# Queries of the opening put off, and unread matmuls in idle array time, in a two-layer transformer prompt kernel

## The chip, the cores and the metric

The kernel runs on one core of one Trainium2 chip. The metric is the time of one execution in device microseconds. All runs quoted here are fast (none was over 1.5% above the fastest of its kernel in its call); a kernel was run several times, and medians are given with their extremes. The calls ran on different chips, so a kernel is compared with the runs of the kernel before that were made beside it, and across calls only by its ratio to those. The granted clock is the share of TensorE's full clock that the profile records.

## The reference, cut to what matters

Two identical layers over x of 2048 x 448 in bfloat16. Each is an attention with 16 heads of 28, over all 2048 keys without a mask, and a dense part of width 1792 with a squared ReLU, each behind a layernorm.

```python
x = x + A(layernorm(x), wqkv, wo)     # softmax(q k^T / sqrt(28)) v, then @ wo
x = x + B(layernorm(x), w1, b1, w2, b2)   # relu(x @ w1 + b1)**2 @ w2 + b2
x = x + A(layernorm(x), wqkv, wo)     # the same weights again
x = x + B(layernorm(x), w1, b1, w2, b2)
```

The softmax needs 2 x 16 x 2048 x 2048 exponentials: 134 million. ScalarE does them all, in 683 instructions of up to 128 x 1536.

## The kernel before

The kernel is written as several streams of operations (scores, exponentials, products with the values, the chain from the attention's output to the next layer's queries), each operation with an engine, an estimated duration and what it depends on. A planner in Python, run when the kernel is built, picks at each step the operation that can start first, and so fixes the order of instructions on each engine. On the chip that order stands, and an engine that comes too early waits: at 186.52 us of the kernel before VectorE has stood 4.23 us before a product whose reciprocals had not landed, and the eviction planned behind it starts at 187.13 us.

```python
LAT = {"PE": 0.22, "ACT": 0.22, "DVE": 0.10, "POOL": 0.15, "DMA": 2.0}

class Planner:
    def run(self):
        ...
            s, _, e, st = min(cands, key=lambda c: (c[0], c[1]))   # earliest start, then priority
            ...
            o.start, o.end = s, s + o.dur
            self.clock[e] = o.end
            if e == "PE":
                self.mode = o.mode
            o.fn(e) if o.fn else None          # emits the instructions
```

A score group is three matmuls of 32 rows (one head each) into a tile of 1536 columns in PSUM, where the kernel puts TensorE's results; the exponential reads the whole tile in one instruction; three matmuls of 32 columns then multiply by the values. There are two such score tiles, one tile of 512 columns, here called a bank, for the attention's output, and one, here called the spare bank, for all other matmuls. The kernel lets a bank take the next result only when another engine has read the last one out; that is called its eviction. At 187.87 us of the kernel before TensorE had waited 3.58 us for one. The streams of scores and exponentials, cut:

```python
def s_stream():
    ...
        o = gbuf[gi]["s"] = Op("PE", 0.23 + 0.04 * mm, fn, deps=list(deps), acq=R_sc, mode="row", sets=("s", gi))
def e_stream():
    ...
        nc.scalar.activation(out=pt[:, 0:n], in_=gbuf[gi]["sc"][:, 0:n], func=AF.Exp, scale=scale)
```

The softmax's denominators of a query block (except the last one of each layer) take a round trip through memory: out to 16 columns per partition, a reciprocal, out to DRAM (`scr<-dn`), and back, spread over the partitions (`rec<-scr`); then VectorE multiplies. The planner holds the last step to take 1.0 us plus 2.0 us until it has landed:

```python
def norm_stream(l, qb, g, res, oe):
    ...
        d1 = Op("DMA", 0.1, spread, deps=[oe])
        r1 = Op("DVE", 0.25, rcp, deps=[d1])
        d2 = Op("DMA", 0.1, away, deps=[r1])
        r = own = Op("DMA", 1.0, back, deps=[d2], acq=R_rec)
    ...
    m = Op("DVE", 0.1 + n / 960, mul, deps=[r], rel=oe)
```

In the opening, blocks of 512 rows of the first layer project keys of one group of heads, all values, the other keys, and then the queries:

```python
        else:
            yield from turned(*ks[0])
            yield from values()
            for a in [*ks[1:], *qs]:
                yield from turned(*a)
        yield Op("DVE", 0.0, None, deps=[last], rel=own_xt)
```

The softmax here doesn't subtract the row's maximum and nothing guards it: scores larger than these inputs give would overflow.

## Time and profile before

| | before |
|---|---|
| median of the first three runs | 1009.54 us (1006.92 to 1010.85) |
| profiled run, span | 1011.8 us |
| exponentials, ScalarE | 683, busy 924.6 us |
| first exponential starts, last ends | 24.1 us, 980.4 us |
| ScalarE waits for scores | 28.6 us in 38 pieces |
| mean granted TensorE clock | 0.895 |

A line of the profile's list of groups gives the source line, the engine, the operation, what is written and read, how often, then busy time and the mean of one, and after the second bar how long the engine stood idle just before these instructions and what ended that. In a timeline a line gives start and length in us, engine, line, operation and count, and in brackets the idle time before it and who ended it. A busy TensorE says little, since its matmuls overlap (four that begin at 697.89 us take 1.89, and the next begin at 699.71); the question is always how long ScalarE, which is the bound with 924.6 us of exponentials in 1011.8, stands idle, and where.

One more view of the kernel before is worth showing, because it shows how short the gaps were where the clock fell. It is the timeline of TensorE as it leaves the first layer's projections behind and has attention alone to do:

```profile
130.97 0.40 PE L502 MATMUL sc<-Q_sb,K_sb 32*128 32x512 bf16 x3 [0.47 <-ACT pt L517]
...
132.32 0.39 PE L502 MATMUL sc<-Q_sb,K_sb 32*128 32x512 bf16 x3 [0.62 <-ACT pt L517]
...
135.00 0.61 PE L502 MATMUL sc<-Q_sb,K_sb 32*128 32x512 bf16 x3 [0.62 <-ACT pt L517]
```

The gaps are 0.47 to 0.62 us, one in each period of about 1.34 us; after four of them the same three matmuls take 0.61 us instead of 0.39. Later, from 843.2 to 872 us, the clock stayed at 0.50 while tiled matmuls of attention alone filled 25.2 of 28.8 us.

### The profile page before, as it was taken

The page shows a single profiled execution, that of the slowest core. Times are in us where ns is not written, and L with a number is a line of the kernel's source. Part 1 is how long each engine was busy: PE and PEld are TensorE (multiplying, and loading weights), DVE is VectorE, ACT ScalarE, POOL GpSimd, SP SyncE. Part 2 cuts the span into 40 slices and gives each one's busy share as a digit, 9 for nine tenths or more (in the row PEclk, how much of TensorE's full clock was granted, in tenths as well). Part 3 has the DMA queues.
Part 4 walks back from the last instruction along what each step waited for, and adds up shares of the span by engine and source line. Part 5 has one row for each costly group of instructions (what it writes and reads, how often), then busy time and mean ns, then how long its engine had stood idle before and what let it go on. Part 6 is the DMA issues. An engine that isn't in the chain of part 4 may idle for free.

```text
span 1011.8 us, 15410 instructions
## 1 busy us (share of the span) xinstructions
PE 907.4 (90%) x6400; PEld 311.0 (31%) x6400; DVE 416.8 (41%) x929; ACT 943.9 (93%) x712; POOL 5.1 (1%) x14
## 2 busy tenths in 40 slices
PE   6989988898988988899898999898898998899998
PEld 2333322233232332233323333222233332233345
DVE  6644425424354154542545514225414510343254
ACT  4999998899999999999999999998899999999982
POOL 2000000000000000000000000000000000000000
PEclk7999967899989989899798998767997996679989
DMA  8000010000000000000000000010000000000000
GB/s 249 15 1 1 1 41 4 12 12 12 12 5 8 13 12 12 1 1 1 1 1 1 1 2 1 12 44 12 12 25 13 6 25 16 18 7 12 15 6 19
DMA packets 19730, 16.72 MB, mean 17 GB/s; under 512 B 8394, under 2 KB 16139, under 8 KB 19660
## 3 DMA queue, kind: packets, MB, share of 16 engines
q1 hardware_dynamic: 19660, 15.74, 5.0%
q8 instruction: 50, 0.82, 0.3%
q14 instruction: 20, 0.16, 0.1%
HBM read 13.47 MB, written 2.05 MB: 15 GB/s over the span
## 4 chain that ended last, share of the span: by engine, by line
ACT 45%; PE 21%; issue 17%; DMA 10%; DVE 6%; SPq 0%; ACTq 0%; DVEq 0%
ACT pt L517 45%; PE mt L385 8%; DMA rec<-scr 6%; PE sc L502 5%; PE oT L548 4%; PE sc L385 2%; DMA scr<-dn 2%; PE tp L350 2%; DMA dn<-oT_sb 1%; DVE r L673 1%; DVE rec L595 1%; DVE oTn L633 1%; DMA x_sb<-in_A_x_dram 1%; DVE K_sb L401 1%; DVE x_sb L644 0%
## 5 line engine op out<-in xcount | busy, mean ns | idle before, releaser
L517 ACT ACTIVATE pt<-sc 128x1536 bf16<-128x1536 f32 (+1 forms) x683 | 924.6, 1517 | 30.3 <-PE sc L502 28.6
L502 PE MATMUL sc<-Q_sb,K_sb 32*128 32x512 bf16 (+1 forms) x2304 | 294.1, 394 | 61.2 <-ACT pt L517 59.8
L548 PE MATMUL oT<-pt,V_sb 128*32 128x512 bf16 (+1 forms) x2304 | 296.1, 400 | 6.0 <-ACT pt L517 3.0
L502 PEld LDWEIGHTS <-K_sb 32*128 32x128 bf16 x2304 | 84.8, 93 | 298.1 <-issue 295.6
L385 PE MATMUL mt<-xnT,w 128*128 128x512 bf16 (+1 forms) x432 | 117.1, 390 | 13.2 <-DVE r L673 7.6
L548 PEld LDWEIGHTS <-V_sb 128*32 128x32 bf16 x2304 | 71.5, 95 | 186.2 <-issue 185.6
L673 DVE TENSOR_SCALAR r<-mt 128x512 bf16<-128x512 f32 x99 | 68.5, 692 | 101.2 <-PE mt L385 101.1
L644 DVE TENSOR_TENSOR x_sb<-x_sb,mt 128x448 bf16<-128x448 bf16 x60 | 37.3, 621 | 169.1 <-PE mt L385 169.1
L385 PE MATMUL mt<-w,h 128*128 128x448 bf16 x406 | 93.7, 356 | 1.3 <-DVE rec L595 0.5
L385 PEld LDWEIGHTS <-w 128*128 128x128 bf16 x504 | 44.0, 100 | 64.6 <-issue 41.3
L385 PEld LDWEIGHTS <-h 128*128 128x128 bf16 x448 | 37.2, 97 | 46.0 <-issue 22.4
L680 DVE TENSOR_TENSOR h<-r 128x512 bf16<-128x512 bf16 x112 | 47.4, 424 | 6.7 <-ACT r L671 3.6
L633 DVE TENSOR_TENSOR oTn<-oT_sb,rec 128x512 bf16<-128x512 f32 (+1 forms) x36 | 22.7, 631 | 63.4 <-DMA rec<-scr 63.2
L299 DVE BATCH_NORM_STATS2 st<-x_sb 128x6 f32<-128x448 bf16 x64 | 38.6, 603 | 1.9 <-DMA x_sb<-in_A_x_dram 1.9
L385 PE MATMUL mt<-xnT,wq 128*128 128x512 bf16 x128 | 34.7, 388 | 2.3 <-DVE K_sb L401 0.5
L401 DVE CAST K_sb<-mt 128x512 bf16<-128x512 f32 x30 | 20.7, 690 | 38.7 <-PE mt L385 38.7
L385 PE MATMUL mt<-wo,oTn 128*128 128x448 bf16 x124 | 33.3, 384 | 3.7 <-DVE oTn L633 2.5
L360 DVE COPY xnT<-tp 128x1024 bf16<-128x1024 bf16 x29 | 20.1, 692 | 37.7 <-PE tp L350 37.5
L401 DVE CAST Q_sb<-mt 128x512 bf16<-128x512 f32 x30 | 20.7, 691 | 34.3 <-PE mt L385 34.3
L385 PE MATMUL mt<-xnT,wk 128*128 128x512 bf16 x120 | 32.6, 381 | 1.9 <-DVE rec L595 0.5
L427 DVE CAST V_sb<-mt 128x448 bf16<-128x448 f32 x29 | 18.1, 625 | 35.7 <-PE mt L385 35.7
L385 PE MATMUL mt<-wv,xnT 128*128 128x448 bf16 x120 | 28.2, 353 | 1.4
(70 smaller groups left out, 311.4 us busy)
## 6 DMA issues: line engine op xcount, KB each, us to landing
rec<-scr SPq DMA_DIRECT2D x24, 256.0 KB
x_sb<-in_A_x_dram SPq DMA_DIRECT2D x8, 224.0 KB
out_dram<-x_sb SPq DMA_DIRECT2D x16, 112.0 KB
w<-in_B_w_dram SPq DMA_DIRECT2D x1, 1568.0 KB
w<-in_B_w_dram SPq DMA_DIRECT2D x1, 1344.0 KB
part_sb<-in_A_wqkv_dram SPq DMA_DIRECT2D x1, 672.0 KB
rec<-scr SPq DMA_DIRECT2D x4, 128.0 KB
wo<-in_A_wo_dram SPq DMA_DIRECT2D x4, 98.0 KB
```

What stands on the lines that cost most here:

```text
L299: nc.vector.bn_stats(out=st[:, :], in_=x_sb[:, t0 + j, :])
L350: nc.tensor.transpose(out=tp[:, dc, k * P:(k + 1) * P], in_=xn[:, dc * P:(dc + 1) * P], identity=ident[:, :])
L360: nc.vector.tensor_copy(out=dst, in_=tp[:, :, 0:w])
L385: nc.tensor.matmul(box["t"][:, c0:c0 + n], lhsT=lhsT, rhs=rhs, start=a, stop=b)
L401: nc.vector.tensor_copy(out=dst, in_=src)
L502: nc.tensor.matmul(sc[:, c0:c0 + nt * P], lhsT=K_sb[l][rows, g, (kb + i) * P:(kb + i + 1) * P], rhs=Q_sb[rows, g, t0 * P:(t0 + nt) * P], s ...
L517: nc.scalar.activation(out=pt[:, 0:n], in_=gbuf[gi]["sc"][:, 0:n], func=AF.Exp, scale=scale)
L548: nc.tensor.matmul(box["t"][DHP * hh:DHP * hh + DHP, 0:n], lhsT=V_sb[l][:, kb + i, 4 * g + hh, :], rhs=gbuf[gi]["pt"][:, c0:c0 + n], start ...
L633: nc.vector.tensor_tensor(out=oTn_of[l, qb][0][:, g, 0:n], in0=res["t"][:, 0:n], in1=box["r"][:, 0:n], op=ALU.mult)
L644: nc.vector.tensor_tensor(out=x_sb[:, tb, :], in0=x_sb[:, tb, :], in1=t[:, 0:D], op=ALU.add)
L673: nc.vector.tensor_scalar(out=r[:, 0:w], in0=t[:, 0:w], scalar1=0.0, scalar2=None, op0=ALU.max)
L680: nc.vector.tensor_tensor(out=h[:, 0:w], in0=r[:, 0:w], in1=r[:, 0:w], op=ALU.mult)
```

## The change

The intent: in the kernel before TensorE's clock is at half in stretches with attention alone (0.50 from 136.0 to 142.8 us, with 5.87 of 6.80 us busy), and the work that follows starts slowly (four matmuls in 1.89 us at 697.89, in 1.04 at 701.70). So idle array time is filled with matmuls whose result nobody reads, wherever the planner's own record of the last 2.8 us shows a load under 0.74. They write to the spare bank, and take the planner's lowest priority, so that they go only where nothing else fits. In the built kernel there are 216 of them. And in the first layer's opening the queries of the three later blocks become a stream of their own, behind keys and values.

```diff
+WINDOW = 2.8
...
+    def load(self, span):
+        now = self.clock["PE"]
+        return sum(e - max(s, now - span) for s, e in self.past if e > now - span) / span
...
             if e == "PE":
                 self.mode = o.mode
+                self.past = [p for p in self.past if p[1] > s - 8.0] + [(s, o.end)]
...
-            for a in [*ks[1:], *qs]:
+            for a in ks[1:]:
                 yield from turned(*a)
-        yield Op("DVE", 0.0, None, deps=[last], rel=own_xt)
+
+            def queries():
+                for a in qs:
+                    yield from turned(*a)
+                yield Op("DVE", 0.0, None, deps=[last], rel=own_xt)
+            if l == 0:
+                pl.spawn(8 + 0.1 * t0, queries())
+            else:
+                yield from queries()
...
+    def heat():
+        for gi in range(1, len(groups)):
+            yield Op("POOL", 0.0, None, deps=[("s", gi)])
+            short = 0.74 - pl.load(WINDOW)
+            if short <= 0:
+                continue
+            k = 1 if short < 0.14 else 2
+
+            def junk(e):
+                t = bank(o, "mt")
+                for _ in range(k):
+                    nc.tensor.matmul(t[:, 0:D], lhsT=ident[:, :], rhs=xns[0][:, 0:D], start=True, stop=True)
+            o = Op("PE", 0.19 * k, junk, deps=[("s", gi)], acq=R_m)
+            yield o
+            yield Op("PE", 0.0, None, deps=[o], rel=o)
...
+    pl.spawn(9.5, heat())
```

More of the change, by code (lines that the diff above doesn't have):

```diff
@@ L61, in __init__ @@
         self.streams = []
+        self.past = []
+    def load(self, span):
+        now = self.clock["PE"]
+        return sum(e - max(s, now - span) for s, e in self.past if e > now - span) / span
     def spawn(self, prio, gen):
@@ L444, in qkv @@
             yield from values()
-            for a in [*ks[1:], *qs]:
+            for a in ks[1:]:
                 yield from turned(*a)
-        yield Op("DVE", 0.0, None, deps=[last], rel=own_xt)
+            def queries():
+                for a in qs:
+                    yield from turned(*a)
+                yield Op("DVE", 0.0, None, deps=[last], rel=own_xt)
+            if l == 0:
+                pl.spawn(8 + 0.1 * t0, queries())
+            else:
+                yield from queries()
     def first_block(blk):
```

## The prediction

Two of its figures for TensorE, from the trace of the kernel before: the 14 matmuls that it takes 189 ns from are those of 448 columns at 988.62 us, which start 189 to 190 ns apart; and its 0.27 us for a set of three tiled matmuls is an estimate, half of the 0.54 us between two sets at half clock (136.35 to 136.89 us).

> **What bounds the kernel now.** I read the page first (shares, clock, the costliest group), then the waits of ScalarE, then tables of short windows for the granted clock, then the timeline around every place where ScalarE stood idle. The page:
>
> ```profile
> PE 907.4 (90%) x6400; PEld 311.0 (31%) x6400; DVE 416.8 (41%) x929; ACT 943.9 (93%) x712; POOL 5.1 (1%) x14
> ...
> PEclk7999967899989989899798998767997996679989
> ...
> L517 ACT ACTIVATE pt<-sc 128x1536 bf16<-128x1536 f32 (+1 forms) x683 | 924.6, 1517 | 30.3 <-PE sc L502 28.6
> ```
>
> ScalarE's 683 exponentials take 924.6 of 1011.8 us. The first starts at 24.1 us, the last ends at 980.4; before that is the opening, after it a tail of 31 us. So the kernel is bound by ScalarE, and all that a change in the middle can win is the idle time before the exponentials. Of it the waits say
>
> ```profile
> ACT pt L517 <- PE sc L502: 28.6, 38, 3.6
> ```
>
> 28.6 us in 38 pieces, all for late scores. With none of them the kernel would need about 981 us; that is the ceiling for the middle. TensorE's 90% is not a limit: its matmuls overlap in this count. The third line to watch is the clock, whose mean is 0.895. Windows (start:end, length, busy us and instructions of PE, PEld, DVE, ACT, POOL, then clock, DMA share, GB/s) show two levels and little between:
>
> ```profile
> 50.00:75.00 25.00, 22.76 (x167) 8.03 (x166) 10.73 (x19) 25.00 (x20) 0.00 (x0) 1.00 0.00 1
> 129.20:136.00 6.80, 4.46 (x36) 1.47 (x32) 2.14 (x4) 6.80 (x7) 0.00 (x0) 0.91 0.07 15
> 136.00:142.80 6.80, 5.87 (x31) 1.53 (x29) 0.85 (x2) 6.80 (x7) 0.00 (x0) 0.50 0.12 36
> 646.00:677.00 31.00, 26.82 (x136) 7.09 (x135) 6.24 (x12) 31.00 (x24) 0.00 (x0) 0.51 0.12 37
> 843.20:872.00 28.80, 25.22 (x184) 7.26 (x181) 1.31 (x3) 28.80 (x23) 0.00 (x0) 0.50 0.04 11
> ```
>
> Half clock comes in stretches with attention alone, and ScalarE is full there (6.80 of 6.80, 31.00 of 31.00, 28.80 of 28.80): half clock costs nothing while nothing else is to be done. It costs afterwards, when the first projections arrive. Two timelines show the two kinds of stall:
>
> ```profile
> 697.89 1.89 PE L385 MATMUL mt<-xnT,w 128*128 128x512 bf16 x4
> 699.71 0.61 PE L502 MATMUL sc<-Q_sb,K_sb 32*128 32x512 bf16 x3
> ...
> 700.42 6.91 ACT L517 ACTIVATE pt<-sc 128x1536 bf16<-128x1536 f32 x5 [1.46 <-PE sc L502]
> ...
> 701.70 1.04 PE L385 MATMUL mt<-xnT,w 128*128 128x512 bf16 x4
> ```
>
> Four matmuls took 1.89 us at half clock and 1.04 us four us later; the scores behind them came 1.46 us late. That is the kind that the change can cure. The other:
>
> ```profile
> 186.52 0.69 DVE L633 TENSOR_TENSOR oTn<-oT_sb,rec 128x512 bf16<-128x512 f32 x1 [4.23 <-DMA rec<-scr]
> 187.13 0.68 DVE L673 TENSOR_SCALAR r<-mt 128x512 bf16<-128x512 f32 x1
> ...
> 187.87 1.01 PE L385 MATMUL mt<-xnT,w 128*128 128x512 bf16 x2 [3.58 <-DVE r L673]
> ...
> 189.53 1.45 ACT L517 ACTIVATE pt<-sc 128x1536 bf16<-128x1536 f32 x1 [3.60 <-PE sc L502]
> ```
>
> VectorE stands 4.23 us before a product whose reciprocals come by DMA; the eviction behind it is held, the one spare PSUM bank stays taken, TensorE waits 3.58 us in order, and ScalarE 3.60 us. No clock cures that.
>
> [...] The trace has 14 such matmuls in 2.81 us; less the 0.35 of a lone one, over 13, that is 189 ns[...], and it prices an added matmul. [...]
>
> **The change, part by part.** Built, the order of the array gains 216 unread matmuls of 448 columns in 140 groups of scores, 76 of them pairs, and as many weight loads. No other work is removed or added; the planner moves the rest by a few groups.
>
> 1. Queries put off. In the opening 12 projection tiles (3 blocks by 4, 48 matmuls) move behind keys and values, from score groups 25 to 77 to groups 26 to 75. I price it at 0: from 32.66 us ScalarE ran 73 exponentials in one piece of 98.27 us, so nothing is to be won there, and the first exponentials hang on block 0, which the change leaves alone.
>
> 2. Fill. 216 x 0.189 = 41 us of array time. In pure attention a period of about 1.345 us holds two sets of three tiled matmuls of about 0.27 us effective each, 0.54 us; one or two fillers add 0.19 to 0.38, leaving at least 0.4 us. So the fill itself costs ScalarE nothing at full clock. By place: 131 of the 216 stand in four stretches with little but attention (groups 75 to 110, 151 to 160, 448 to 485, 576 to 606), and most of the rest in the gaps of layernorm, where the clock also fell.
>
> What it can cure, from the 38 stalls one by one:
> - clock alone (at 294, 296, 414, 416, 499, 501, 550, 697, 700, 779, 892, 894, 979): 0.35 + 0.62 + 0.35 + 0.34 + 0.35 + 0.56 + 0.35 + 0.35 + 1.46 + 1.05 + 0.35 + 1.46 + 0.90 = 8.5 us;
> - output projection after a long stretch, late data and clock together (155, 158, 678, 874, 876), 4.9 us in all, of which I take 3.0, what half-rate matmuls added;
> - VectorE held by a DMA or a long reciprocal (189, 191, 193, 308, 312, 397, 399, 430, 435, 464, 467, 686, 727, 732): 13.8 us, none;
> - 1.4 us of crumbs, none.
>
> So 11.5 us, and each cured restart saves 0.1 us more (a lone exponential is 1.45 us against a spacing of (98.27 - 1.45)/72 = 1.345): 15 x 0.1 = 1.5. Together 13.0 us. The fill is set by the planner's load of 0.74 at planned times, so some drops will stay; I choose 0.7: 9.1 us.
>
> 3. Tail. The clock was 0.66 to 0.84 from 972 to 986; two sets of eight matmuls took 1.89 and 1.81 us instead of 1.04, so a full clock wins 1.6 us. But in the new order the last block but one does its second output projection 4 score groups before the end instead of 8, and its transposes and first 16 hidden-layer matmuls move behind the last scores: 16 x 0.12 = 1.9 us and some wait for layernorm, 3 us by estimate. Net loss 1.4.
>
> Sum: 1009.5 - 9.1 + 1.4 = 1001.8; I put 1001.5.
>
> **The rivals.** (a) The clock is not held: tiled matmuls may count for little[...] and fillers at 15 to 28% of the time may be too few. For it: those long stretches. Against: layernorm gaps that sometimes passed at 1.00. Then nothing is won, and fillers of 0.37 us at half clock push 1.08 us of attention per period over 1.345: 1009 to 1014. (b) The stalls behind VectorE take the place of those cured: 13.8 us stay, and moved orders could add two or three of 2 to 3.6 us; products with DMA behind them still stand amid hidden-layer evictions in the new order. About 1007. (c) Everything goes well, and VectorE's holds fall in better places too: 990 to 994. (d) A filler takes the spare bank, and TensorE must wait there for VectorE's eviction; the new VectorE order has the last eviction ahead of the held product wherever I looked, so I give it little.
>
> **Range and chances.** Before spread over 1006.9 to 1010.9. With (b) above and (c) below I take 993 to 1008. Over 2% faster means under 989.4, which needs 20 of the 28.6 us: 0.06. Over 2% slower needs rival (a) at its worst and more: 0.02.
>
> **What would show it.** Mean clock up from 0.895 to about 0.95 or more, 1.00 in the three stretches shown at half; ScalarE's wait for scores from 28.6 to about 18 us, the pieces of 1.46 gone and those of 2 to 4 us behind reciprocals still there; 683 exponentials at near 915 us busy; last exponential near 971 us, tail about 32 us. A clock still at 0.50 in the long stretches makes step 2 wrong; a full clock with waits unchanged makes my sorting of stalls wrong; a first exponential more than 2 us away from 24.1 makes step 1 wrong.

## The result, and the profile after

| | before | changed |
|---|---|---|
| median | 1009.7 us (1006.92 to 1010.85, 4 runs) | 992.23 us (991.45 to 994.68, 4 runs) |
| profiled span | 1011.8 us | 989.5 us |
| first exponential starts, last ends | 24.1, 980.4 us | 23.7, 958.2 us |
| from there to the end | 31.4 us | 31.4 us |
| ScalarE waits for scores | 28.6 us, 38 pieces | 11.3 us, 18 pieces |
| mean granted clock | 0.895 | 0.991 |

The ratio of the two is 0.9835, with a 95% interval of 0.9808 to 0.9862. Ratios here and below are the mean time of one kernel's fast runs over that of the other's of the same rounds, so not quite the ratio of the medians quoted. The measured time lies 0.8 us under the low end of the predicted range and 9.3 us under the predicted time: the gain was 17.5 us where 8 were forecast. The two profiled runs lie further apart than the medians: 1013.62 us, above all four quoted for the kernel before, and 991.45 us, the fastest of the changed kernel's. Their spans differ by 22.3 us, so the terms read off this pair below add up to more than 17.5.

The page of the changed kernel, in the lines that answer to those shown of the one before: engines, clock by slices of the span, and the exponentials.

```profile
PE 893.7 (90%) x6562; PEld 317.6 (32%) x6616; DVE 415.3 (42%) x927; ACT 942.3 (95%) x714; POOL 5.1 (1%) x14
...
PEclk7999999999999999999999999999999999999999
...
L534 ACT ACTIVATE pt<-sc 128x1536 bf16<-128x1536 f32 (+1 forms) x683 | 921.3, 1535 | 11.7 <-PE sc L519 11.3
```

Everything after the opening reads 9, and the exponentials' own busy time fell by 3.3 us, since a restart costs about 0.1 us (1.45 us for a lone exponential, 1.345 from start to start in a row) and there are 31 fewer (24 and not 55, counted in the traces with the short pauses that the list of waits leaves out). The windows of the stretches that were at half clock (columns as in the prediction; places moved, since the kernel is faster):

```profile
136.00:142.80 6.80, 5.91 (x40) 2.02 (x39) 1.55 (x3) 6.80 (x6) 0.00 (x0) 1.00 0.11 34
634.00:664.00 30.00, 27.35 (x174) 7.52 (x171) 7.63 (x15) 30.00 (x23) 0.00 (x0) 1.00 0.13 38
825.00:852.00 27.00, 22.46 (x194) 8.15 (x191) 1.19 (x3) 27.00 (x21) 0.00 (x0) 1.00 0.02 5
```

All three are at 1.00, and ScalarE is as full there as it was. The timeline at the place of the 1.46 us stall, where the second layer's hidden matmuls of a block begin:

```profile
684.47 1.02 PE L393 MATMUL mt<-xnT,w 128*128 128x512 bf16 x3
685.43 0.39 PE L519 MATMUL sc<-Q_sb,K_sb 32*128 32x512 bf16 x3
...
685.92 5.48 ACT L534 ACTIVATE pt<-sc 128x1536 bf16<-128x1536 f32 x4 [0.22 <-PE sc L519]
```

1.02 us instead of 1.89 (one of the four matmuls has no record; its weight load has), and 0.22 us of ScalarE instead of 1.46. And the place where VectorE had been held for 4.23 us and ScalarE for 3.60, which I had written off:

```profile
183.55 0.69 DVE L650 TENSOR_TENSOR oTn<-oT_sb,rec 128x512 bf16<-128x512 f32 x1 [1.18 <-DMA rec<-scr]
184.16 0.68 DVE L690 TENSOR_SCALAR r<-mt 128x512 bf16<-128x512 f32 x1
...
184.89 1.02 PE L393 MATMUL mt<-xnT,w 128*128 128x512 bf16 x4 [0.50 <-DVE r L690]
```

The hold is 1.18 us, TensorE waits 0.50, and ScalarE not at all. This I had not foreseen.

I numbered the exponentials and sorted the waits of the changed kernel as the prediction had sorted those of the kernel before, by place and by what TensorE was waiting for:

| kind of stall (my sorting) | before | predicted to go | changed |
|---|---|---|---|
| clock alone | 8.5 us | 0.7 x 8.5 = 6.0 | 0.6 |
| output projection after a long stretch, mixed | 4.9 | 0.7 x 3.0 = 2.1 | 3.3 |
| VectorE held by a DMA or a long reciprocal | 13.8 | 0 | 6.3 |
| crumbs, and one stall made by the fill | 1.4 | 0 | 1.1 |
| sum | 28.6 | 8.1 | 11.3 |

The sum of 17.3 us that went is 7.9 us in the first kind, 1.6 in the second, and 7.5 in the third, for which I had put zero.

### The profile page after: what moved, and what is told of

Its sections match the earlier page's. It is cut to its first block, busy times and chain, and to the rows that moved or that the text cites. A ratio compares the mean times of both kernels' runs of the same rounds, so it can differ in the third digit from the quotient of the medians.

```text
span 989.5 us, 15799 instructions
## 1 busy us (share of the span) xinstructions
PE 893.7 (90%) x6562; PEld 317.6 (32%) x6616; DVE 415.3 (42%) x927; ACT 942.3 (95%) x714; POOL 5.1 (1%) x14
## 4 chain that ended last, share of the span: by engine, by line
ACT 44%; issue 18%; PE 16%; DMA 13%; DVE 7%; SPq 0%; ACTq 0%; DVEq 0%
ACT pt L534 44%; DMA rec<-scr 9%; PE mt L393 8%; PE sc L519 3%; DMA scr<-dn 3%; PE oT L565 3%; PE sc L393 2%; DVE r L690 1%; DVE oTn L650 1%; DMA dn<-oT_sb 1%; PE mt L733 1%; DVE x_sb L661 1%; DMA x_sb<-in_A_x_dram 1%; DVE K_sb L409 1%; DVE st L307 0%
## 5 line engine op out<-in xcount | busy, mean ns | idle before, releaser
L534 ACT ACTIVATE pt<-sc 128x1536 bf16<-128x1536 f32 (+1 forms) x683 | 921.3, 1535 | 11.7 <-PE sc L519 11.3
L519 PE MATMUL sc<-Q_sb,K_sb 32*128 32x512 bf16 (+1 forms) x2304 | 268.1, 359 | 42.8 <-ACT pt L534 32.3
L565 PE MATMUL oT<-pt,V_sb 128*32 128x512 bf16 (+1 forms) x2304 | 266.8, 365 | 6.6 <-ACT pt L534 3.2
L393 PE MATMUL mt<-xnT,w 128*128 128x512 bf16 (+1 forms) x392 | 105.4, 371 | 11.4 <-DVE r L690 3.0
L393 PE MATMUL mt<-w,h 128*128 128x448 bf16 x420 | 96.5, 357 | 2.8 <-DVE x_sb L661 1.5
L733 PE MATMUL mt<-xn,ident 128*128 128x448 bf16 x216 | 68.5, 357 | 7.0 <-DVE xnT L368 2.8
L393 PEld LDWEIGHTS <-w 128*128 128x128 bf16 x504 | 43.5, 97 | 55.3 <-issue 31.2
L650 DVE TENSOR_TENSOR oTn<-oT_sb,rec 128x512 bf16<-128x512 f32 (+1 forms) x36 | 22.8, 633 | 72.4 <-DMA rec<-scr 72.2
L393 PE MATMUL mt<-wo,oTn 128*128 128x448 bf16 x124 | 30.8, 361 | 5.3 <-DVE oTn L650 3.2
L588 DVE COPY oT_sb<-oT 128x512 f32<-128x512 f32 (+1 forms) x26 | 15.8, 607 | 44.0 <-PE oT L565 43.9
L393 PE MATMUL mt<-xnT,wk 128*128 128x512 bf16 x107 | 31.2, 380 | 2.3
```

The source lines that it names most:

```text
L393: nc.tensor.matmul(box["t"][:, c0:c0 + n], lhsT=lhsT, rhs=rhs, start=a, stop=b)
L519: nc.tensor.matmul(sc[:, c0:c0 + nt * P], lhsT=K_sb[l][rows, g, (kb + i) * P:(kb + i + 1) * P], rhs=Q_sb[rows, g, t0 * P:(t0 + nt) * P], s ...
L565: nc.tensor.matmul(box["t"][DHP * hh:DHP * hh + DHP, 0:n], lhsT=V_sb[l][:, kb + i, 4 * g + hh, :], rhs=gbuf[gi]["pt"][:, c0:c0 + n], start ...
L650: nc.vector.tensor_tensor(out=oTn_of[l, qb][0][:, g, 0:n], in0=res["t"][:, 0:n], in1=box["r"][:, 0:n], op=ALU.mult)
L733: nc.tensor.matmul(t[:, 0:D], lhsT=ident[:, :], rhs=xns[0][:, 0:D], start=True, stop=True)
```

## The experiments

Every kernel was correct. "Beside" means the runs of the kernel before on the same chip.

### The new order without the fill

This is the changed kernel with the unread matmuls planned but not issued. On TensorE it is the changed kernel less the 216 matmuls and their weight loads, on VectorE it is the same row by row.

```diff
             def junk(e):
+                return
                 t = bank(o, "mt")
```

> The new order of every instruction on every engine, with the 216 unread matmuls not issued (the planner still counts their time). Theory A (the fill acts through the clock, and a full clock also shortened the times that VectorE was held by the reciprocals' DMA): back to 1004 to 1011 us, mean clock about 0.90, ScalarE's wait for scores 25 to 30 us. Rival B (the new order, not the clock, removed the stalls behind VectorE): 994 to 999 us with a clock of about 0.90, ScalarE's wait 12 to 18 us.

Measured: 1010.01 us (1009.06 to 1014.03) beside 1010.6; ratio 1.0009 (0.9968 to 1.0050); clock 0.908 in the profile. ScalarE's waits for scores were 23.4 us, a little under the 25 to 30 of theory A. Lines of the page:

```profile
PEclk8999968998989999799897998958998995789989
...
L534 ACT ACTIVATE pt<-sc 128x1536 bf16<-128x1536 f32 (+1 forms) x683 | 924.4, 1516 | 25.3 <-PE sc L519 23.4
```

So the order gives nothing that these runs show; rival B of that run falls, and the whole gain needs the matmuls to run. The same place in the timeline as above, now in the changed kernel's own order but without fill:

```profile
184.98 0.69 DVE L650 TENSOR_TENSOR oTn<-oT_sb,rec 128x512 bf16<-128x512 f32 x1 [3.25 <-DMA rec<-scr]
...
186.33 1.02 PE L393 MATMUL mt<-xnT,w 128*128 128x512 bf16 x4 [2.57 <-DVE r L690]
...
188.00 2.96 ACT L534 ACTIVATE pt<-sc 128x1536 bf16<-128x1536 f32 x2 [2.35 <-PE sc L519]
```

The hold is back at 3.25 us, so it looked as if the full clock had shortened it; theory A had said so. But against that stood a sum: VectorE's waits for that DMA were 72.5 us in this run and 72.2 us in the changed kernel. By these sums the clock does not shorten the holds on the whole. What it did at this one place is settled by the last two experiments. The tail, from the last exponential to the end, was 33.4 us here, against 31.4 before and 31.4 in the changed kernel: in these profiles the new order costs 2.0 us there, and the fill gives 2.0 back.

### The queries alone, and the fill alone

Queries alone is the change without the line that starts the fill; fill alone is the change without the separate stream of queries (the plan then has 222 unread matmuls).

```diff
-    pl.spawn(9.5, heat())                 # queries alone
```

```diff
-            if l == 0:                    # fill alone
-                pl.spawn(8 + 0.1 * t0, queries())
-            else:
-                yield from queries()
+            yield from queries()
```

> The queries put off, no fill and no room planned for it. My step 1 priced this at 0: 1007 to 1012 us, clock 0.88 to 0.91. Rival: the opening matters: 1000 to 1005 us.

> The fill alone, queries where they were before. Theory A: 990 to 995 us, clock 0.98 or more, as the whole change. If the queries' move carries part of the gain, 997 us or more.

> The fill alone, a second time, because its four runs went from 991.7 to 1005.2 us with clocks of 0.993 to 0.974. If the queries' move matters only as noise: the same as the control within 2 us. If the older order of queries leaves the fill less able to hold the clock: 3 us or more above the control, with clocks below 0.985 in the slow runs.

> The changed kernel once more, as control beside the next three: 991 to 996 us, clock 0.985 to 0.992.

Measured: queries alone 1013.1 us (1011.18 to 1014.52) beside 1010.6, ratio 1.0036 (0.9993 to 1.0080). Fill alone, first call: 1000.12 us, from 991.69 to 1005.18, ratio 0.9895 (0.9832 to 0.9957). Fill alone, second call, on another chip: 990.91 us (989.92 to 994.98) beside the changed kernel at 991.16 (991.02 to 991.52); ratios to before 0.9843 and 0.9839.

So the queries' move is worth nothing that these runs show, as step 1 of the prediction had it, and the fill makes the gain. The first call's spread stays open: its four runs had clocks of 0.993, 0.983, 0.974 and 0.976 and times of 991.7, 998.7, 1005.2 and 1001.6 us, so in three of them the clock was lost in places. The changed kernel was never run on that chip; whether the chip or the older order of queries makes the hold on the clock weaker, I did not settle.

### Where the fill matters

Both kernels have the order of the changed kernel. The first leaves out unread matmuls of the four stretches in which attention waits for the softmax's denominators; the second leaves out all others. My count in the first expectation is wrong: the number in the condition is the one that the fill's stream has got to, which can lie behind the score groups. In the built programs 81 of 216 are left out in the first (24, 5, 13 and 39 in the four stretches; 22 at the beginning of the third stay) and the other 135 in the second.

```diff
             def junk(e):
+                if 75 <= gi < 94 or 151 <= gi < 158 or 448 <= gi < 467 or 576 <= gi < 606:   # second: if not (...)
+                    return
                 t = bank(o, "mt")
```

> Order of the changed kernel; no unread matmuls in the four waiting stretches (score groups 75 to 93, 151 to 157, 448 to 466, 576 to 605; 112 of 216 left out), all others kept. Theory: half clock costs nothing inside such a stretch and only the stalls just after it come back, some 3 to 6 us: 994 to 999 us, clock 0.92 to 0.95. Rival: losing the clock there spoils what follows for long: 1002 us or more.

> The complement: unread matmuls in the four waiting stretches alone, none in the gaps of layernorm and elsewhere. Theory: the larger part of the gain belongs to those gaps: 1000 to 1007 us, clock 0.93 to 0.96, with 1.00 in the long stretches and 0.5 to 0.7 in the layernorm gaps. Rival: the long stretches carry the gain: 993 to 998 us.

Measured, with the changed kernel at 991.16 us: without fill in the long stretches 993.18 us (988.92 to 995.90), ratio to before 0.9854 (0.9801 to 0.9907); fill in the long stretches alone 1006.83 us (1004.36 to 1008.16) beside 1006.04, ratio 0.9990 (0.9945 to 1.0036). A window in the last long stretch of each, first without and then with fill there:

```profile
825.00:852.00 27.00, 23.61 (x172) 6.82 (x169) 0.94 (x2) 27.00 (x21) 0.00 (x0) 0.50 0.04 12
```

```profile
835.00:862.00 27.00, 22.58 (x187) 7.90 (x184) 1.27 (x3) 27.00 (x21) 0.00 (x0) 0.96 0.02 6
```

and what ScalarE waited for scores in each, in the same order:

```profile
ACT pt L534 <- PE sc L519: 11.7, 21, 1.6
```

```profile
ACT pt L534 <- PE sc L519: 18.4, 34, 1.5
```

At half clock the first kernel's ScalarE is full through all 27 us, and its whole run keeps nearly all of the gain with a mean clock of 0.96. The second has a mean clock of 0.93, well above the 0.895 of before, and its four times show no gain over the seven beside them. The mean clock is not what pays. What pays is the fill outside the long stretches: of the 135 unread matmuls that the first kernel keeps, 94 stand between the first statistics of a layernorm and the copy of its turned result, just before a dense stretch begins. That it is these 94 alone was not tested.

The second kernel's zero is a net result, though. In two stretches its clock had fallen before the fill took hold, and there the unread matmuls ran at half rate and made the scores late:

```profile
660.00:672.00 12.00, 11.77 (x48) 2.00 (x47) 2.35 (x5) 8.80 (x7) 0.00 (x0) 0.50 0.11 34
```

```profile
665.29 1.14 PE L735 MATMUL mt<-xn,ident 128*128 128x448 bf16 x2
...
667.08 1.45 ACT L534 ACTIVATE pt<-sc 128x1536 bf16<-128x1536 f32 x1 [0.71 <-PE sc L519]
```

The array was busy for 11.77 of 12 us, and the clock stayed at 0.50; two unread matmuls took 1.14 us, where two at 127.69 us of the changed kernel took 0.54. Such pieces (133.9 to 139.4 and 661.2 to 671.4 us) make 4.3 of the 18.4 us that ScalarE waited, while the stalls right behind two of the stretches, those at 155, 158, 874 and 876 us before, are gone. So fill in the long stretches did help somewhere, and lost it again: it kept the clock at 0.96 in the last one, but did not bring it back within the 12 us from 660 to 672.

### How much fill

Fewer: one unread matmul at each place. More: one more at each. Narrow: the same 216, 64 columns wide instead of 448. The texts count 140 places, 76 of them pairs, and so 140 and 356 unread matmuls for fewer and more; the traces hold 163 and 379. The places are 163, some of them between the same two exponentials, and fewer leaves out 53.

```diff
-                for _ in range(k):
+                for _ in range(1):            # fewer;   more: range(k + 1)
```

```diff
-                    nc.tensor.matmul(t[:, 0:D], lhsT=ident[:, :], rhs=xns[0][:, 0:D], ...)
+                    nc.tensor.matmul(t[:, 0:64], lhsT=ident[:, :], rhs=xns[0][:, 0:64], ...)   # narrow
```

> The changed kernel with one unread matmul at each of the 140 places instead of one or two (76 fewer), same order. If the fill has margin: 991 to 995 us, clock 0.98 or more. If it just suffices: 996 to 1004 us, clock 0.92 to 0.96, with 0.50 again in the long stretches.

> The changed kernel a third time, as control for the next three and to see whether another chip gives the spread of 991 to 1005 us that the fill alone had in its first call: 991 to 995 us if it does not matter.

> One unread matmul at each of 140 places, again (first call 1001.8 us, clock 0.964, without a control beside it). If the dose matters: 4 us or more above the control, clock lower by 0.02. If it was that chip: within 2 us of the control.

> One more unread matmul at each of the 140 places (356 in all), planned time and order as in the changed kernel. At full clock a period of 1.345 us then holds 0.54 us of attention and at most 0.57 of fill, so ScalarE should not notice: within 2 us of the control, clock as there or up to 0.995. Rival: over-filling delays scores: 3 us or more above.

> The changed kernel with its 216 unread matmuls 64 columns wide instead of 448: same number, same order, about a seventh of the array time. If what holds the clock is the share of time in which the array streams: back to 1004 to 1010 us, clock 0.90 to 0.93. If the number of matmuls is enough: 991 to 995 us, clock 0.98 or more.

Measured: fewer, first call, 1001.8 us (998.83 to 1006.57), ratio 0.9924 (0.9879 to 0.9970); second call, on another chip, 995.55 us (993.44 to 1000.91), ratio 0.9861 (0.9812 to 0.9911), beside the changed kernel at 992.63 us (991.45 to 993.13), ratio 0.9823. More: 996.22 us (994.59 to 997.58), ratio 0.9861 (0.9813 to 0.9909), clock 0.993 in every run. Narrow: 1022.76 us (1021.74 to 1024.48) beside 1009.98, ratio 1.0137 (1.0115 to 1.0160), clock 0.892.

With fewer, the clock varied from run to run (0.964 to 0.990 over both calls, where the changed kernel's runs had 0.984 to 0.991) and the time with it. The second call lies 2.9 us above its control, between the two answers of its expectation (under 2, and 4 or more). With more, I had expected no cost, and that was wrong. The timeline of a long stretch shows why:

```profile
651.98 1.15 PE L733 MATMUL mt<-xn,ident 128*128 128x448 bf16 x4
653.06 0.39 PE L519 MATMUL sc<-Q_sb,K_sb 32*128 32x512 bf16 x3
...
653.38 0.40 PE L565 MATMUL oT<-pt,V_sb 128*32 128x512 bf16 x3
653.56 1.45 ACT L534 ACTIVATE pt<-sc 128x1536 bf16<-128x1536 f32 x1 [0.28 <-PE sc L519]
...
653.71 1.15 PE L733 MATMUL mt<-xn,ident 128*128 128x448 bf16 x4
```

Unread matmuls stood four in a row for 1.15 us ahead of a score group, and each such exponential came 0.28 us late. The starts in that timeline give the sum that I had wrong: from the scores to the products 0.32 us and from there to the unread matmuls 0.33, so 0.65 for attention and not 0.54; the four take 1.08 us until the next scores, 0.27 each and not 0.19. Together 1.73 us, more than the 1.345 us of an exponential. The narrow ones show that the number of matmuls alone does not hold the clock here: 216 of them left the clock at 0.892, and cost 1.4% besides. A narrow one at half clock still takes its place in the order, 0.29 us for two:

```profile
133.01 0.61 PE L565 MATMUL oT<-pt,V_sb 128*32 128x512 bf16 x3
133.56 0.29 PE L733 MATMUL mt<-xn,ident 128*128 128x64 bf16 x2
```

ScalarE's waits for scores rose to 33.2 us in 49 pieces there.

### The product placed later

The trace shows that the last DMA of the reciprocals lands about 5 us after its issue, not 3: at the 24 places of the kernel before where VectorE was held for one by over 0.3 us, the product began 4.8 to 5.3 us after the issue (181.35 to 186.52 us, for one). I told the planner, in the changed kernel, in the kernel before, and in the changed kernel with its fill not issued.

```diff
-            r = own = Op("DMA", 1.0, back, deps=[d2], acq=R_rec)
+            r = own = Op("DMA", 3.0, back, deps=[d2], acq=R_rec)
```

> The changed kernel with the planner told that the last DMA of the reciprocals takes 5 us to land instead of 3 (the trace shows about 5), so that it puts the product that needs them later on VectorE; the number of unread matmuls follows the new plan (221). If the waits left to ScalarE (11.3 us) stem from VectorE held before that product: 983 to 988 us, ScalarE's wait for scores under 7 us, VectorE's wait for that DMA under 45 us instead of 72. If they stem from elsewhere: 989 us or more.

> The kernel before, with only the planner's landing time of the reciprocals' last DMA at 5 us instead of 3; no fill, queries as before. If the stalls behind VectorE (13.8 us by my count) are independent of the clock: 993 to 999 us, clock about 0.90. If a full clock is needed as well: 1003 us or more.

> The fill and the later product together (979.4 us), less the unread matmuls, in the same order. The fill without VectorE's holds to help with. If the fill cured what I sorted as stalls of the clock alone (13 us with restarts) plus the tail (1.6 to 2): 992 to 996 us, clock about 0.90. If part of its gain was in stalls behind VectorE, it is worth less here: 985 to 990 us. If the fill is worth still more: 997 us or more.

Measured: with fill 979.36 us (977.79 to 980.89) beside 1011.83, ratio 0.9693 (0.9653 to 0.9733). This version beats both kernels; it is 13 us faster than the changed kernel of the same call (992.63). The kernel before, alone with this: 1001.93 us (997.71 to 1003.34) beside 1009.98, ratio 0.9922 (0.9893 to 0.9951). The new order with this and no fill: 993.05 us (989.56 to 997.10), ratio 0.9844 (0.9804 to 0.9885). The third lies in the first band of its expectation, 992 to 996. The second falls between the two answers of its own (993 to 999, and 1003 or more), so it does not decide whether the stalls behind VectorE depend on the clock. ScalarE's and VectorE's waits with fill:

```profile
DVE oTn L650 <- DMA rec<-scr: 58.6, 18, 6.6
...
ACT pt L534 <- PE sc L519: 2.6, 6, 0.6
```

VectorE is still held for 58.6 us, against the under 45 that I expected, but hardly ever with an eviction behind it that TensorE needs: ScalarE's wait falls to 2.6 us. With that, the fill can be weighed twice, each time in one order, as a difference of ratios to the kernel before:

| | fill off | fill on | worth of the fill |
|---|---|---|---|
| product where it was | 1.0009 | 0.9823 to 0.9839 | 1.7 to 1.9%, 17 to 19 us |
| product later | 0.9844 | 0.9693 | 1.5%, 15 us |

Each ratio carries some 0.4% of uncertainty and each difference some 0.6%, or 6 us, so the two rows do not differ for certain. What the second row shows is that the fill is worth some 9 to 21 us with few stalls behind VectorE for it to act on. That agrees with the whole of what I had counted as curable (13.0 us in the middle and 1.6 in the tail), but also with 0.7 of the middle and 1.6, which is 10.7. The two profiles of that row differ by 11.7 us in span: ScalarE's waits for scores are 9.6 and 2.6 us, and the tail is 31.2 and 31.5 us, so there the fill gains nothing in the tail. One thing is left open here: with the product later and no fill, the new order is 0.8% faster than the order of before, while with the product where it was the two are equal. The planned but empty room for the fill seems to help once the holds are gone; I have not shown how.

### What had held VectorE at 189 us

In the kernel before and in the new order without fill, the small write of the reciprocals ahead of that hold took 3.13 and 3.25 us; in the changed kernel it took 1.42. I then measured these writes, 28 in a run, in eleven of the traces. Nearly all take 1.39 to 1.48 us, but for the second one (1.8 to 2.7 in each run) and the twelfth (1.9 in each), unless a 16 KB transfer of the queue called instruction begins in their window; of the 26 with such a transfer 23 took 2.0 to 3.6 us. Of the others eight took 1.5 to 2.0 us, for which I have no reason. The list of queues of the kernel before, in the 3.13 us of that write, has one:

```profile
q8 instruction: 1, 0.02, 2.8%
```

There are 50 such transfers in a run before and 51 with the fill. The profile before has 12 800 matmuls and weight loads of TensorE, and 226 to 288 of them begin between one transfer and the next; so I put one transfer at 256 of TensorE's instructions, an estimate from 12 800 and 50. By that the fill, which adds 432, may just have moved the transfers; one begins at 178.92 us in the kernel before, in that write's window, while the nearest of the changed kernel begin at 171.69 and 191.53. To test it without touching the clock, I put narrow matmuls among those at the very start of the kernel before: 64, which are 128 instructions and by the estimate half a transfer, and 128, which are a whole one.

```diff
         for _ in range(WARM):
             nc.tensor.matmul(idle[:, 0:D], lhsT=b2w[:, 0:P], rhs=b2w[:, :], start=True, stop=True)
+        for _ in range(64):                   # control: 128
+            nc.tensor.matmul(idle[:, 0:16], lhsT=b2w[:, 0:P], rhs=b2w[:, 0:16], start=True, stop=True)
```

> The kernel before with 64 more unread matmuls of 16 columns among those at its very start, nothing else. They are 128 more TensorE instructions[...]. If the long hold at 189 us (5.0 us of ScalarE) comes from such a transfer that meets the small write of the reciprocals (3.13 us instead of 1.4): that write takes 1.4 us, the stall there is under 1.5 us, unless another site is met; time 1003 to 1007 us, clock unchanged at about 0.90. If the half clock makes the hold: it stays.

> The same with 128 more matmuls, 256 instructions[...]. If the transfers matter: the write near 178 us takes about 3 us again and the stall of 3 to 5 us is there; 1007 to 1012 us. If the work added at the start matters: as the run with 64.

Measured: with 64, 1004.63 us (1004.19 to 1009.74) beside 1009.8, ratio 0.9965 (0.9937 to 0.9994); with 128, 1010.79 us (1007.48 to 1011.47), ratio 1.0004 (0.9979 to 1.0029). The clock was 0.898 and 0.894. The queue's timeline and ScalarE after it, where the time of the write is the step from the start of the first line to that of the second; first with 64, then with 128:

```profile
176.28 0.32 SPq L618 DMA_DIRECT2D scr<-dn  x1
177.70 0.52 SPq L625 DMA_DIRECT2D rec<-scr  x1
...
184.84 2.79 ACT L519 ACTIVATE pt<-sc 128x1536 bf16<-128x1536 f32 x2 [0.84 <-PE sc L504]
```

```profile
177.77 0.32 SPq L618 DMA_DIRECT2D scr<-dn  x1
181.02 0.53 SPq L625 DMA_DIRECT2D rec<-scr  x1
...
188.77 1.45 ACT L519 ACTIVATE pt<-sc 128x1536 bf16<-128x1536 f32 x1 [3.27 <-PE sc L504]
```

The 64 take the write to 1.42 us and the stall from 5.0 us (with the two that follow it) to 1.0; with 128 both are back, at 3.25 us and 4.9 us. The list of queues has no such transfer in the write's window with 64 (176.28 to 177.70 us), and one between 170 and 184 us with 128. So the half clock alone does not make that hold: at mean clocks of 0.898 and 0.894 the write took 1.42 us without a transfer and 3.25 with one. The narrow fill agrees, with the same 432 instructions more and a clock of 0.892: there the write took 1.42 us, and ScalarE stood 0.24 us at 189.6. The changed kernel has the same trouble elsewhere: its write at 351.6 us took 2.73 us with a transfer in its window, and ScalarE stood 1.15 us at 361.9; in its two other profiled runs that write took 3.0 and 3.1 us and cost 3.6 to 3.9 us in all. Some of the 7.5 us in the table above is therefore luck of one profile.

## Why the prediction was wrong, point by point

**What bounds the kernel.** Right. ScalarE's waits for scores fell from 28.6 to 11.3 us, and the kernel's time with them. That these 17.3 us are so near to the 17.5 of the medians is chance, since the two profiled runs are 22.3 us apart.

**Step 1, the queries at 0.** Right: 1.0036 (0.9993 to 1.0080) alone, and the first exponential starts 0.4 us from where it did.

**Step 2, the fill.** What the fill does to the clock was right: with it the clock was 0.991 and the stalls of the clock alone went from 8.5 to 0.6 us; in the same order without it the clock was 0.908 and the time that of before. The price of the fill was right in what came of it and wrong in its working. In pure attention it cost ScalarE nothing, and half clock there cost nothing either, as the run without fill in those stretches shows. But the room that two unread matmuls leave in a period is about 0.2 us (1.345 less 0.65 less 0.48 for a pair, from 127.69 to the next scores at 128.17 us in the changed kernel) and not 0.4, and one more at each place overfilled it. The size was too small, and one term that was mis-sized is the factor: "some drops will stay; I choose 0.7". Of the 11.5 us counted, 8.1 were to go, and 9.5 went in the profiles. I had taken a guess at how well the author's threshold was set for a number, where no view of the kernel before could give one. Another is the restarts: they were to save 0.7 x 1.5 = 1.05 us, and the exponentials' own time fell by 3.3.

**Step 2, VectorE held at "none".** This is the step that failed by most, for a reason that I had not thought of. In the profiles 7.5 of 13.8 us went. Of this 5.0 us are the stall at 189 us, and they came with an instruction transfer in the small write's window: with one the write took 3.13 to 3.25 us, without one 1.42, also at a mean clock of 0.892 and 0.898. The added instructions moved it away; the clock did not cure it. "No clock cures that" holds at this place, and the zero is still wrong, by luck: the new places of the transfers happened to spare this write. The rest, some 2.5 us, is in the order of what differs between two runs of the same kernel (the changed kernel's three profiles wait 11.3, 11.3 and 14.3 us for scores).

**Step 3, the tail.** The sizes were nearly right: 2.0 us lost by the order for 3 estimated, 2.0 won with the fill for 1.6. Together 0 and not minus 1.4.

**The rivals.** (a) did not happen in the changed kernel, but it did in two stretches of the run with fill in the long stretches alone, where scores came 0.24 to 0.71 us late at half clock. (d) happened once in this profile: an unread matmul at 681.7 us waited 1.16 us for the spare bank behind a held VectorE, and cost 0.65 us. (c), which the range of 993 to 1008 left out but for its last microsecond, was nearest in time; that VectorE's holds fell in better places is half true, by the transfer at 189 us.

**The signs.** The clock, the long stretches and the missing pieces of 1.46 us came as said. The pieces of 2 to 4 us behind the reciprocals, which were to stay, are missing in this profile; one of 2.4 or 2.5 us came back in each of the changed kernel's two others. Two signs could not have come, by the prediction's own numbers: 683 exponentials at a spacing of 1.345 us are 918.6 us busy and not near 915 (921.3 measured), and 28.6 less 8.1 leaves 20.5 us of waits and not about 18 (11.3 measured).

By terms: the profiled pair is 22.3 us apart, 14.6 more than the 7.7 worked out. Of these, 7.5 lie in the stalls behind VectorE, 2.2 in the restarts, 1.5 in the tail, 1.4 in the factor; the other 2.0 are crumbs, other pauses of ScalarE and the earlier start. The medians are only 17.5 us apart, so some 4.8 of the 14.6 are owed to which runs were profiled, and I cannot say in which term. What is shown is the largest single piece, 5.0 us at 189 us; how much else of the gain behind VectorE is luck and how much the fill's doing stays open.

## What to carry to other kernels

When TensorE has slack beside another engine that is the bound, ask what its clock is at the moment at which dense work begins, not on average: the 135 full-width unread matmuls outside the long slack stretches, most of them just ahead of it, gave nearly all of 1.6%, and the 81 inside gave nothing on balance. Fill before the clock falls: where it came too late, the array stood full (11.77 us busy) at half clock for 12 us and the fill delayed scores. Fill by array time and not by count (216 unread matmuls of 448 columns gave a clock of 0.991, of 64 columns 0.892), measure both sides of the dose, and do not let fill stand ahead of the matmul that the bound engine waits for (four in a row made the exponential 0.28 us late). Profile each kernel more than once before a difference is shared out among its terms. And give a planner that fixes the order of an engine the landing times that the trace shows: one constant, 3 us instead of 1, was worth 13 us more.
